# Windowed attention with a fused feed-forward product: attention row tiles by head pair, sums in one phase, and another order of the first loads

## The chip, the cores and the metric

One core of one Trainium2 chip runs the whole program. The metric is the device time of one execution in microseconds (us). "Span" is the length of the profiled execution, which is 1 to 2 us below the time of the same execution.

## The reference

Attention in a window of 32 tokens on either side, for 8 batches of 8 heads with 576 tokens of 64 elements, and then a feed-forward block over all 4,608 tokens:

```python
def _attn_ref(q, k, v):                                  # (8, 8, 576, 64) each
    scores = scale * np.matmul(q, k.transpose(0, 1, 3, 2))
    mask = np.abs(pos[:, None] - pos[None, :]) <= 32
    scores = np.where(mask, scores, -1000000000.0)
    ...                                                  # softmax over the last axis
    return np.matmul(attn, v)

def _moe_ref(x, w_in, w_out):                            # x (4608, 512), w_in (512, 2048), w_out (2048, 512)
    h = x @ w_in
    g = np.where(h >= 1, h, np.where(h <= -1, 0.0, (h + 1) ** 2 / 4.0))
    return g @ w_out
```

`x` is the output of the attention with the heads side by side, so no row of the first product can start before the attention of its token is done.

## The kernel before

The program is a list of steps in a fixed order. Step `a` computes one eighth (256 columns) of the first product for a tile of 256 tokens, `hp`; ScalarE and VectorE turn it into `gT`; and `LAG` steps later four matmuls of the second product, `op`, use it. The eight batches' attention is put between `hp` and `op` of chosen steps. There are 144 steps with an `hp`, and `LAG` more that have only `op`.

Q and K must have their 64 elements on the partitions. For batch 0 rows of nine tokens are loaded ("long" rows) and transposed on TensorE; for all others rows of one token are loaded and the DMA engines transpose them:

```python
    def load_long(b, qd):                     # 9 tokens of 64 elements in a run
        for src, dst, nm in ((q, qn, "qn"), (k, kn, "kn")):
            ...
            nc.gpsimd.dma_start(out=dst[b][:, qd], in_=rows.rearrange("h (x j) d -> x h (j d)", j=NC))

    def load_nat(b, t):                       # one token of 64 elements in a run
        ...
        for h in range(2):
            nc.gpsimd.dma_start(out=x[:, :, h], in_=src[b, NY * h:NY * h + NY].rearrange("y s d -> (y s) d")
                                .rearrange("(u p) d -> p u d", p=128))

    def xpose(b, t):                          # transpose by DMA
        nc.sync.dma_start_transpose(out=..., in_=(qn, kn)[t][b].rearrange("p u h d -> p (u h d)"))
    ...
    load_long(0, 0)
    load_long(0, 1)
    load_nat(0, 2)
    load_w_in(0, 512)
    load_w_in(512, DFF)
    for t in range(3):
        load_nat(1, t)
    for n in range(4):
        load_w_out(n)
    ...
    loads, xps = {}, {7: [(1, 0)], 8: [(1, 1)]}          # batch 1's DMA transposes in steps 7 and 8
```

The weighted sums of V (`nm`) and the row sums (`dn`) are made of 64x64 matmuls, with the two halves of the partitions ("row tiles") adding into the same PSUM banks. So they go in two phases, and a VectorE copy of one element (`scr`) keeps the second phase behind the first:

```python
    def part(ps, col):
        nc.vector.tensor_copy(scr[64:65, 0:1], ps[64:65, col:col + 1])
    ...
        def phase(first):
            s = list(sums(0 if first else 1, first))
            ...
            for f in s[:2] + list(rows(1 if first else 0, first)) + s[2:]:
                f()
            if first:
                part(nm, hi - lo - 1)
```

A step, in program order:

```python
        # the sums' first phase stands before hp if the step has no scores, else after it
        hp = ps_h.tile([128, 2, TB], FP, name="hp", tag="hp")
        for j in range(2):
            for kk in range(4):
                nc.tensor.matmul(hp[:, j], w_in[...], xT[:, kk, r0:r0 + TB], start=kk == 0, stop=kk == 3)
        nc.scalar.activation(rr, hp, AF.Relu, scale=0.5, bias=0.5)
        nc.vector.tensor_max(hp, hp, rr)
        nc.vector.scalar_tensor_tensor(gT[t][:, 2 * f:2 * f + 2], rr, 1.0, hp, op0=ALU.min, op1=ALU.mult)
        # scores of a later head, the sums' second phase, ln and exp of the row sums
        for x in range(4 * (a - LAG), 4 * (a - LAG) + 4):
            nc.tensor.matmul(op, gT[...], w_out[:, ff], ...)
```

The softmax here doesn't subtract the row's maximum and nothing guards it: scores larger than these inputs give would overflow.

Of the kernel before, what the change touches and what calls it, by code (L numbers as in the profile page):

```python
# [15 lines left out]
def kernel(  # L16
# [19 lines left out]

# [9 lines left out]
    PAD = 32  # L46

    const = ctx.enter_context(tc.tile_pool(name="const", bufs=1))
    nat = ctx.enter_context(tc.tile_pool(name="nat", bufs=2))
    ktp = ctx.enter_context(tc.tile_pool(name="ktp", bufs=3))  # L50
    ptp = ctx.enter_context(tc.tile_pool(name="ptp", bufs=5))
    pt8p = ctx.enter_context(tc.tile_pool(name="pt8p", bufs=2))
# [3 lines left out]
    osp = ctx.enter_context(tc.tile_pool(name="osp", bufs=2))  # L56
    ps_h = ctx.enter_context(tc.tile_pool(name="ps_h", bufs=2, space=bass.MemoryType.PSUM))
    ps_o = ctx.enter_context(tc.tile_pool(name="ps_o", bufs=2, space=bass.MemoryType.PSUM))
    ps_s = ctx.enter_context(tc.tile_pool(name="ps_s", bufs=2, space=bass.MemoryType.PSUM))
    ps_n = ctx.enter_context(tc.tile_pool(name="ps_n", bufs=1, space=bass.MemoryType.PSUM))  # L60
    ps_d = ctx.enter_context(tc.tile_pool(name="ps_d", bufs=1, space=bass.MemoryType.PSUM))
# [4 lines left out]
    mask4 = const.tile([128, 512], BF, name="mask4")  # L66
    mask8 = const.tile([128, 2 * TAIL], BF, name="mask8")
# [6 lines left out]
    V, P = nc.vector, nc.gpsimd  # L74
# [4 lines left out]
    def load_long(b, qd):  # L79

        for src, dst, nm in ((q, qn, "qn"), (k, kn, "kn")):
            if qd == 0:
                dst[b] = nat.tile([128, 2, 2, S], BF, name=nm, tag=nm)
            rows = src[b].rearrange("(h y) s d -> h (y s) d", h=2)[:, 2 * qd * S:2 * qd * S + 2 * S]
            nc.gpsimd.dma_start(out=dst[b][:, qd], in_=rows.rearrange("h (x j) d -> x h (j d)", j=NC))

    def load_nat(b, t):
        src, dst, nm = ((q, qn, "qn"), (k, kn, "kn"), (v, vn, "vn"))[t]
        x = dst[b] = nat.tile([128, NU, 2, D], BF, name=nm, tag=nm, bufs=3 if t == 2 else 2)
        for h in range(2):  # L90
            nc.gpsimd.dma_start(out=x[:, :, h], in_=src[b, NY * h:NY * h + NY].rearrange("y s d -> (y s) d")  # L91
                                .rearrange("(u p) d -> p u d", p=128))

    def load_w_in(f0, f1):
        f = slice(f0, f1)
        for h in range(2):
            nc.gpsimd.dma_start(out=w_in[64 * h:64 * h + 64, :, f],
                                in_=moe_w_in.rearrange("(h y d) f -> h d y f", h=2, d=64)[h][:, :, f])
# [5 lines left out]
    nc.scalar.preload_act_table_set("natural_log_exp_and_others")  # L104
    load_long(0, 0)
    make_identity(nc, ident)

    nc.gpsimd.memset(mask1, 1.0)
    for h in range(2):
        r = slice(64 * h, 64 * h + 64)  # L110
        nc.gpsimd.affine_select(out=mask1[r], in_=mask1[r], compare_op=ALU.is_ge, fill=0.0, base=0,
                                channel_multiplier=-1, pattern=[[1, 128]])
        nc.gpsimd.affine_select(out=mask1[r], in_=mask1[r], compare_op=ALU.is_ge, fill=0.0, base=64,
                                channel_multiplier=1, pattern=[[-1, 128]])
    load_long(0, 1)
    nc.vector.memset(ones, 1.0)
    for t in qTs:
        nc.vector.memset(t[:, 0:PAD], 0.0)
    for m, n, w in ((mask4, 4, 128), (mask8, 2, TAIL)):
        nc.vector.tensor_copy(m.rearrange("p (n j) -> p n j", n=n),  # L120
                              mask1[:, 0:w].rearrange("p (n j) -> p n j", n=1).to_broadcast([128, n, w]))
    load_nat(0, 2)
    load_w_in(0, 512)
    load_w_in(512, DFF)
    for t in range(3):
        load_nat(1, t)
    for n in range(4):
        load_w_out(n)


    qj, kj, kT = {}, {}, {}

    def relay(b, qd, t, eng):

        src, dst, nm = ((qn, qj, "qj"), (kn, kj, "kj"))[t]
        if qd == 0:
            dst[b] = gtp.tile([128, 2, NC, 2, D], BF, name=nm, tag="gT")
        eng.tensor_copy(dst[b][:, qd].rearrange("p j h d -> p h j d"),
                        src[b][:, qd].rearrange("p h (j d) -> p h j d", d=D))

    def qT(b):
        return qTs[b % 3][:, PAD:]

    def tpose(b, qd, t, part, copy):

        if t == 1 and b not in kT:
            kT[b] = ktp.tile([128, NY * S], BF, name="kT")
        j0, j1 = ((0, 5), (5, 9))[part]
        src = (qj, kj)[t][b]
        ps = ps_h.tile([128, 5, 128], BF, name="tp", tag="hp")  # L150
        for j in range(j0, j1):
            nc.tensor.transpose(ps[:, j - j0], src[:, qd, j].rearrange("p h d -> p (h d)"), ident)
        o = qT(b) if t == 0 else kT[b]
        copy(o.rearrange("d (y p j) -> d y p j", p=64, j=NC)[:, 2 * qd:2 * qd + 2, :, j0:j1],
             ps[:, :j1 - j0].rearrange("d j (g p) -> d g p j", g=2))

    def xpose(b, t):

        if t == 1:
            kT[b] = ktp.tile([128, NY * S], BF, name="kT")  # L160
        o = qT(b) if t == 0 else kT[b]
        nc.sync.dma_start_transpose(out=o.rearrange("d (u p) -> d u p", p=128),  # L162
                                    in_=(qn, kn)[t][b].rearrange("p u h d -> p (u h d)"))
# [3 lines left out]
    def half(n):  # L167
        return slice(64 * (n % 2), 64 * (n % 2) + 64)

    HD = (slice(0, 64), slice(64, 128))  # L170

    def scores(i, eng):
        b, y = divmod(i, NY)
        p = pt[i] = ptp.tile([128, 2, 512], BF, name="pt")
        ps = [ps_s.tile([128, 512], FP, name="sc", tag="sc") for _ in range(2)]
        for c in range(8):
            for h in range(2):
                nc.tensor.matmul(ps[h][half(NC * y + c), 128 * (c // 2):128 * (c // 2) + 128],  # L178
                                 kT[b][HD[h], S * y + 64 * c:S * y + 64 * c + 64],
                                 qTs[b % 3][HD[h], PAD + S * y + 64 * c - 32:PAD + S * y + 64 * c + 96],  # L180
                                 start=True, stop=True)
        for h in range(2):
            nc.scalar.activation(p[:, h], ps[h], AF.Exp, scale=D ** -0.5)  # L183
            eng.tensor_mul(p[:, h], p[:, h], mask4)  # L184

    def scores8(b, eng):
        p = pt8[b] = pt8p.tile([128, 2, 2 * TAIL], BF, name="pt8")
        ps = [ps_s.tile([128, 512], FP, name="sc", tag="sc") for _ in range(2)]
        for y in range(NY):
            for h in range(2):  # L190
                nc.tensor.matmul(ps[h][half(y), TAIL * (y // 2):TAIL * (y // 2) + TAIL],
                                 kT[b][HD[h], S * y + 512:S * y + 576],
                                 qTs[b % 3][HD[h], PAD + S * y + MAIN:PAD + S * y + S], start=True, stop=True)
        for h in range(2):
            nc.scalar.activation(p[:, h], ps[h][:, :2 * TAIL], AF.Exp, scale=D ** -0.5)
            eng.tensor_mul(p[:, h], p[:, h], mask8)

    def mm(o, w, x, **kw):
        return nc.tensor.matmul(o, w, x, skip_group_check=True, **kw)  # L199

    scr = const.tile([128, 8], FP, name="scr")

    def part(ps, col):

        nc.vector.tensor_copy(scr[64:65, 0:1], ps[64:65, col:col + 1])  # L205

    muls, spare = [], [False]

    def banks(alt):
        if alt and spare[0]:  # L210
            nm, dn = (ps_o.tile([128, 512], FP, name=n, tag="op") for n in ("nm", "dn"))
        else:
            nm, dn = ps_n.tile([128, 512], FP, name="nm"), ps_d.tile([128, 512], FP, name="dn")
        spare[0] = not spare[0]
        return nm, dn

    def finish_pv(nm, dn, n, out_ap, shape):
        lr = smp.tile([128, MAIN], FP, name="lr", bufs=1)
        rc = smp.tile([128, MAIN], FP, name="rc")
        nc.scalar.activation(lr[:, :n], dn[:, :n], AF.Ln)  # L220
        nc.scalar.activation(rc[:, :n], lr[:, :n], AF.Exp, scale=-1.0)  # L221
        muls.append(lambda: nc.vector.tensor_mul(out_ap, shape(nm[:, :n]), shape(rc[:, :n])))  # L222

    def pv(i, lo=0, hi=MAIN, alt=False):

        b, y = divmod(i, NY)
        nm, dn = banks(alt)
        def sums(par, first):
            R = half(y + par)
            n = 0  # L230
            for c2 in range(4):
                q0, q1 = 128 * c2 - 32 + 64 * par, 128 * c2 + 96 + 64 * par
                a0, a1 = max(0, q0, lo), min(q1, hi)
                if a0 >= a1:
                    continue
# [224 lines left out]
```

## Time and profile before

| | before |
|---|---|
| time, median (lowest to highest of 4) | 363.94 us (363.13 to 365.18) |
| span | 362.0 us |
| first `hp` | 26.98 us |
| step 10 begins | 67.24 us |
| step 143, the last with an `hp`, begins | 343.97 us |
| mean granted clock of TensorE, as the profile has it | 0.971 |

The profile's clock records begin only at 40.5 us in this run. The mean above and the row `PEclk` count the time before as full speed, although the first eight `hp` matmuls took 1.89 us there and 1.05 later: early on, read the clock from the matmuls' own times.

The prediction below reads the slices, the waits and the timeline. Beside them, this is the page's first part (busy time of each engine, its share of the span, its instructions) and the two VectorE groups that every step has (line, engine, operation, shapes and count, then busy time and mean ns, then the idle time before them and what ended it):

```profile
PE 303.8 (84%) x3227; PEld 202.6 (56%) x3268; DVE 245.1 (68%) x410; ACT 190.6 (53%) x353; POOL 124.7 (34%) x127
...
L409 DVE TENSOR_TENSOR hp<-hp,rr 128x512 f32<-128x512 f32 x144 | 100.7, 699 | 43.4 <-ACT rr L408 40.3
L410 DVE SCALAR_TENSOR_TENSOR gT<-rr,hp 128x512 bf16<-128x512 f32 x144 | 98.8, 686 | 5.0
```

TensorE is busy 84% of the span, but that average hides two stretches: the slices show it nearly full from 85 us on and half idle before. VectorE needs 0.699 + 0.686 = 1.385 us for every step, while TensorE needs 1.735 in a step without attention.

### The profile page before, as it was taken

Reading aid. Unit: us, or ns where it says so; the run is one execution under the profiler, and the core shown is the slowest. Engines: PE = TensorE matmul, PEld = TensorE weight load, DVE = VectorE, ACT = ScalarE, POOL = GpSimd, SP = SyncE. Lnnn points to the kernel's source line nnn. Section 1 sums busy time; section 2 is a strip of 40 time slices with the busy share of each in tenths; the row PEclk is TensorE's granted clock in tenths of the full one; section 3 lists DMA queues with packets and bytes.
Section 4 is the critical chain, followed back from the end, with each engine's and each line's share of the span. In section 5 each row is a group of like instructions: output and inputs, shape, how many; then the busy total and the mean of one; then the engine's idle time right before and its main releaser. Section 6 shows DMA issues by size and latency. Waiting matters only on the chain.

```text
span 362.0 us, 7810 instructions
## 1 busy us (share of the span) xinstructions
PE 303.8 (84%) x3227; PEld 202.6 (56%) x3268; DVE 245.1 (68%) x410; ACT 190.6 (53%) x353; POOL 124.7 (34%) x127
## 2 busy tenths in 40 slices
PE   1555830649999999999999999999999999999995
PEld 1333520336666666666666666666666666666642
DVE  2554660385788777778787877877878777788730
ACT  2464320373766657555655667567556665534421
POOL 8834121000963258313921394159313421000000
PEclk9999995598999999999999999999999999999999
DMA  7999999990998019970995099829940000100011
GB/s 105 177 193 151 124 175 92 139 163 0 88 166 165 31 49 152 117 161 29 134 190 94 29 147 111 189 38 130 181 101 32 30 31 31 56 34 29 32 72 72
DMA packets 144292, 36.54 MB, mean 101 GB/s; under 512 B 135553, under 2 KB 139137, under 8 KB 144257
## 3 DMA queue, kind: packets, MB, share of 16 engines
q0 software_dynamic: 106368, 18.35, 72.6%
q1 hardware_dynamic: 37888, 17.70, 25.0%
q8 instruction: 25, 0.41, 0.5%
q14 instruction: 11, 0.08, 0.1%
HBM read 36.70 MB, written 9.44 MB: 127 GB/s over the span
## 4 chain that ended last, share of the span: by engine, by line
PE 62%; DMA 14%; POOL 9%; DVE 5%; issue 4%; ACT 3%; SPq 2%; ACTq 0%; POOLq 0%
PE op L422 29%; PE hp L400 27%; DMA kT<-kn 9%; DMA qn<-in_q_dram 5%; PE nm L199 4%; SPq L162 2%; POOL vn L91 2%; POOL pt L184 2%; DVE hp L409 2%; POOL qn L91 2%; ACT rr L408 2%; DVE gT L410 1%; POOL kn L91 1%; DVE scr L205 1%; PE dn L199 1%
## 5 line engine op out<-in xcount | busy, mean ns | idle before, releaser
L400 PE MATMUL hp<-xT,w_in 128*128 128x256 bf16 x1152 | 155.2, 280 | 3.4 <-DVE gT L410 3.4
L408 ACT ACTIVATE rr<-hp 128x512 f32<-128x512 f32 x144 | 86.0, 597 | 115.4 <-PE hp L400 108.2
L422 PE MATMUL op<-w_out,gT 128*128 128x512 bf16 x535 | 138.5, 379 | 4.9 <-issue 4.1
L400 PEld LDWEIGHTS <-w_in 128*128 128x128 bf16 x1152 | 113.7, 100 | 48.6 <-DVE gT L410 6.0
L409 DVE TENSOR_TENSOR hp<-hp,rr 128x512 f32<-128x512 f32 x144 | 100.7, 699 | 43.4 <-ACT rr L408 40.3
L410 DVE SCALAR_TENSOR_TENSOR gT<-rr,hp 128x512 bf16<-128x512 f32 x144 | 98.8, 686 | 5.0
L184 POOL TENSOR_TENSOR pt<-pt,mask 128x512 bf16<-128x512 bf16 x48 | 54.6, 1161 | 117.0 <-ACT pt L183 117.0
L422 PEld LDWEIGHTS <-gT 128*128 128x128 bf16 x576 | 53.8, 98 | 42.6 <-issue 0.4
L183 ACT ACTIVATE pt<-sc 128x512 bf16<-128x512 f32 x64 | 34.7, 594 | 22.8 <-PE sc L178 22.6
L199 PE MATMUL nm<-pt,vn 64*64 64x128 bf16 (+2 forms) x656 | 33.8, 224 | 15.4 <-DVE xT L222 11.7
L199 PEld LDWEIGHTS <-vn 64*64 64x64 bf16 x656 | 24.0, 113 | 27.7 <-issue 25.5
L222 DVE TENSOR_TENSOR xT<-nm,rc 128x480 bf16<-128x480 f32 (+3 forms) x44 | 25.8, 592 | 19.7 <-ACT rc L221 15.6
L199 PE MATMUL dn<-pt,ones 64*64 64x64 bf16 (+5 forms) x272 | 33.1, 304 | 1.1 <-DVE xT L222 0.4
L178 PE MATMUL sc<-qT,kT 64*64 64x128 bf16 x512 | 14.8, 234 | 18.9 <-DMA kT<-kn 17.1
L426 ACT COPY osb<-op 128x512 f32<-128x512 f32 x36 | 21.0, 583 | 16.9 <-PE op L422 16.9
L221 ACT ACTIVATE rc<-lr 128x480 f32<-128x480 f32 (+3 forms) x44 | 24.3, 552 | 1.4
L178 PEld LDWEIGHTS <-kT 64*64 64x64 bf16 x512 | 12.4, 116 | 20.6 <-DMA kT<-kn 17.5
L220 ACT ACTIVATE lr<-dn 128x480 f32<-128x480 f32 (+3 forms) x44 | 23.1, 525 | 0.3
L91 POOL DMA_DIRECT2D kn<-in_k_dram x14 | 17.1, 1232 | 14.3 <-DMA vn<-in_v_dram 13.8
L91 POOL DMA_DIRECT2D vn<-in_v_dram x16 | 19.6, 1239 | 3.9 <-DMA w_out<-in_moe_w_out_dram 3.7
L184 DVE TENSOR_TENSOR pt<-pt,mask 128x512 bf16<-128x512 bf16 x16 | 6.5, 422 | 18.4 <-ACT pt L183 18.1
L91 POOL DMA_DIRECT2D qn<-in_q_dram x14 | 17.3, 1242 | 1.9 <-DMA kn<-in_k_dram 1.2
(33 smaller groups left out, 66.8 us busy)
## 6 DMA issues: line engine op xcount, KB each, us to landing
out_dram<-osb SPq DMA_DIRECT2D x36, 256.0 KB, 2.1
qn<-in_q_dram POOLq DMA_DIRECT2D x16, 288.0 KB, 6.8
kn<-in_k_dram POOLq DMA_DIRECT2D x16, 288.0 KB, 8.2
vn<-in_v_dram POOLq DMA_DIRECT2D x16, 288.0 KB, 10.2
w_out<-in_moe_w_out_dram POOLq DMA_DIRECT2D x4, 512.0 KB, 31.2
w_in<-in_moe_w_in_dram POOLq DMA_DIRECT2D x2, 768.0 KB, 13.5
w_in<-in_moe_w_in_dram POOLq DMA_DIRECT2D x2, 256.0 KB, 8.4
qT<-qn SPq DMA_TRANSPOSE x7, 5.1
```

What stands on the lines that cost most here:

```text
L91: nc.gpsimd.dma_start(out=x[:, :, h], in_=src[b, NY * h:NY * h + NY].rearrange("y s d -> (y s) d") .rearrange("(u p) d -> p u d", p=128))
L178: nc.tensor.matmul(ps[h][half(NC * y + c), 128 * (c // 2):128 * (c // 2) + 128], kT[b][HD[h], S * y + 64 * c:S * y + 64 * c + 64], qTs[b % ...
L183: nc.scalar.activation(p[:, h], ps[h], AF.Exp, scale=D ** -0.5)
L184: eng.tensor_mul(p[:, h], p[:, h], mask4)
L199: return nc.tensor.matmul(o, w, x, skip_group_check=True, **kw)
L221: nc.scalar.activation(rc[:, :n], lr[:, :n], AF.Exp, scale=-1.0)
L222: muls.append(lambda: nc.vector.tensor_mul(out_ap, shape(nm[:, :n]), shape(rc[:, :n])))
L400: nc.tensor.matmul(hp[:, j], w_in[:, kk, 256 * f + 128 * j:256 * f + 128 * j + 128], xT[:, kk, r0:r0 + TB], start=kk == 0, stop=kk == 3)
L408: nc.scalar.activation(rr, hp, AF.Relu, scale=0.5, bias=0.5)
L409: nc.vector.tensor_max(hp, hp, rr)
L410: nc.vector.scalar_tensor_tensor(gT[t][:, 2 * f:2 * f + 2], rr, 1.0, hp, op0=ALU.min, op1=ALU.mult)
L422: nc.tensor.matmul(op, gT[tt // 2][:, ff, 128 * (tt % 2):128 * (tt % 2) + 128], w_out[:, ff], start=ff == 0, stop=ff == 2 * NF - 1)
```

## The change

The intent is fourfold.

1. A row tile now belongs to a head pair (`a`), and each pair has its own PSUM bank. No bank is shared by row tiles, so the sums go in one phase, without the VectorE copy.
2. Batch 1's Q and K come in runs of nine tokens and are transposed on TensorE. Batches 0 and 1 are loaded by halves of their tokens, the first half of batch 0 as fp32 from the SP and ScalarE queues. Batch 2 is transposed on TensorE too. DMA transposes start with batch 3.
3. `LAG` falls from 14 to 10, and attention visits are placed anew.
4. Matmuls on zeros fill TensorE's idle time in the start, to keep its clock up.

Smaller edits come with these: a visit (a step's share of attention) now takes 224 or 256 tokens of four heads instead of 480 tokens of two, one exponential covers 1,024 columns instead of 512, and some of the first ten `hp` use the banks of `op`.

```diff
-    load_long(0, 0)
+    q32, k32 = (early.tile([128, 2, S], FP, name=nm) for nm in ("q32", "k32"))
+    load_long(0, 0, 0, nc.sync, q32)
+    load_long(0, 0, 1, nc.scalar, k32)
 ...
-    load_nat(0, 2)
-    load_w_in(0, 512)
-    load_w_in(512, DFF)
-    for t in range(3):
-        load_nat(1, t)
-    for n in range(4):
-        load_w_out(n)
+    load_v(0)
+    load_w_in(0)
+    load_long(0, 1, 0)
+    load_long(0, 1, 1)
+    for n in range(1, 4):
+        load_w_in(n)
+    load_w_out(0)
+    load_long(1, 0, 0)
+    load_long(1, 0, 1)
+    load_w_out(1)
+    load_v(1)
+    load_w_out(2)
+    load_w_out(3)
+    load_long(1, 1, 0)
+    load_long(1, 1, 1)
 ...
-    def part(ps, col):
-        nc.vector.tensor_copy(scr[64:65, 0:1], ps[64:65, col:col + 1])
 ...
+    def sums(b, y1, lo, hi, pool=ps_n):
+        bb = two_banks(pool)                  # [128, 2, 512] fp32: one bank per head pair a
+        ...
+        for n, (c, c0, c1, p) in enumerate(todo):
+            o = D0 if c is None else 0
+            for a in range(2):
                 for h in range(2):
+                    nc.tensor.matmul(bb[HD[h], a, o + c0:o + c1], ones[HD[a]] if c is None else vn[b][HD[a], c, h],
+                                     p(a, h), start=n == 0, stop=True, skip_group_check=True)
 ...
+    def keep_warm(n, pool, tag):
+        z = pool.tile([128, 512], FP, name="z", tag=tag)
+        for _ in range(n):
+            nc.tensor.matmul(z, warm[:, :128], warm, start=True, stop=True)
 ...
-    LAG = 14
+    LAG = 10
 ...
+    at(2, None, (0, (0, 1), (0, 2), (2, 4)))          # scores alone
+    at(3, None, (0, (1, 2), (0, 2), (2, 4)))
+    at(4, None, (0,))
+    at(5, (0, 0, TB, MAIN), None)                     # sums alone
+    at(6, (0, 1, TB, MAIN), None)
+    at(7, (0, 0, MAIN, S), None)
 ...
+    for a, b, half in ((0, 0, 1), (8, 1, 0), (15, 1, 1)):         # transposes on TensorE
+        for t in range(2):
+            tps[a + t] = [(b, 2 * half + part, t) for part in range(2)]
+    for n in range(3):
+        tps[20 + n] = [(2, n, t) for t in range(2)]
```

## The prediction

> **What bounds the kernel now.** The kernel is one core. Each of its 144 steps makes a 256-column piece of the first matmul (8 matmuls, `hp`), turns it into `gT` on ScalarE and VectorE, and, some steps later, does 4 matmuls of the second product (`op`). Attention for later batches is slipped between `hp` and `op`. I first read the page's 40 slices (9.05 us each).
>
> ```profile
> PE   1555830649999999999999999999999999999995
> ...
> PEclk9999995598999999999999999999999999999999
> DMA  7999999990998019970995099829940000100011
> GB/s 105 177 193 151 124 175 92 139 163 0 88 166 165 31 49 152 117 161 29 134 190 94 29 147 111 189 38 130 181 101 32 30 31 31 56 34 29 32 72 72
> ```
>
> From slice 10 (about 85 us) TensorE is full; before it TensorE is half idle while DMA is full, and the granted clock halves in slices 7 and 8. So there are two regimes. The waits and the chain of waits name the first; the TensorE timeline dates it.
>
> ```profile
> PE sc L178 <- DMA kT<-kn: 17.1, 2, 16.3
> ```
>
> ```profile
> 12.71 17.75 DMA qn<-in_q_dram
> 30.54 7.34 SPq L162
> 38.00 28.62 DMA kT<-kn
> ```
>
> ```profile
> 26.98 1.89 PE L400 MATMUL hp<-xT,w_in 128*128 128x256 bf16 x8
> ...
> 49.31 1.05 PE L400 MATMUL hp<-xT,w_in 128*128 128x256 bf16 x8 [0.81 <-DVE gT L410]
> 66.66 0.64 PE L178 MATMUL sc<-qT,kT 64*64 64x128 bf16 x16 [16.31 <-DMA kT<-kn]
> ```
>
> The reader sees: the first `hp` starts at 26.98 and at half speed (1.89 against 1.05 us); ten steps are done by 51; then 16.3 us pass until the DMA transpose of batch 1's K, itself 28.6 us long among other loads, lands. The first `op` comes at 84.6. At 85.60 begins the sixteenth step, at 344.13 the last: 128 steps in 258.5 us. A step without attention takes 0.87 + 0.865 = 1.735 us, 222 us for 128. The remaining 36.5 us belong to 31 attention visits, some 1.15 each. One of them:
>
> ```profile
> 95.32 1.04 PE L400 MATMUL hp<-xT,w_in 128*128 128x256 bf16 x8
> ...
> 96.29 0.23 PE L199 MATMUL nm<-pt,vn 64*64 64x96 bf16 x2
> ...
> 96.51 0.40 PE L178 MATMUL sc<-qT,kT 64*64 64x128 bf16 x16
> ...
> 96.77 0.16 DVE L205 COPY scr<-nm 1x1 f32<-1x1 f32 x1
> ...
> 96.98 0.22 PE L199 MATMUL nm<-pt,vn 64*64 64x64 bf16 x2
> ...
> 97.53 0.81 PE L422 MATMUL op<-w_out,gT 128*128 128x512 bf16 x3 [0.16 <-issue]
> ...
> 98.18 1.04 PE L400 MATMUL hp<-xT,w_in 128*128 128x256 bf16 x8
> ```
>
> From `hp` to `hp` 2.86, so attention costs 1.12: 0.10 between `hp` (ends 96.19) and the first sums, 0.22 first phase, 0.2 scores, then until 96.98 the second phase waits for the one-element VectorE copy `scr` (ends 96.93), about 0.25; then 0.2 of sums and about 0.13 back to `op` (one `op` record is missing). Only about 0.65 of 1.12 is streaming.
>
> **What the Trainium skill says.** "TensorEngine Tiling (Array Packing)", Gotcha 1: row tiles that share a PSUM bank must be kept apart by software; and, under Key Properties, changing the tiling mode drains the array. The trace agrees: the `scr` copy is that separation, and the gaps of 0.10 and 0.13 lie at the mode changes. "TensorE: Matmul & The Clock Gate", Part 1: the array runs at half clock until it has been busy some 3.4 us, and again after idling as long. The trace agrees in effect: eight `hp` matmuls take 1.89 at 27 us, 1.05 from 42 us on, and again 1.89 after the stall. "DMA: Bandwidth & Descriptors", Specifications: under 512 bytes per piece the line rate is missed. The windows agree: 217 GB/s from 18 to 20 us when weights load, 148 from 98 to 100 us when Q, K and V load in 64-element rows.
>
> **The change part by part.**
>
> *Loads.* Batch 1's Q and K now come in runs of nine tokens and are transposed on TensorE; so do batch 0's, the first half as fp32 from the SP and ScalarE queues at once. Batch 2 is transposed on TensorE too. In written bytes, at 215 GB/s for wide rows and 150 for token rows: fp32 half 3 us (1.18 MB, my estimate at the read rate of the cast loads, twice 215), V of batch 0 3.9, first w_in quarter 2.4, second half of Q and K 2.7, rest of w_in 7.3, w_out in four parts 9.8, batch 1's Q and K 5.5, its V 3.9: 38.5 us. From 2 us that ends at 41. Before, token-wise batches 1 and 2 and four DMA transposes came into the same stretch. The last of it, batch 1's second half, is wanted at step 15. So the 16.3 us stall should go.
>
> *Start.* Halves land at about 5 us; cast (0.7), transposes (0.7), copies (0.75), the same for K, put the first scores near 10 us; three exponentials (1.0, 0.6, 1.0; one 512-wide takes 0.59) and masks (0.7) end near 13.4; sums, logarithm, exponential (0.6 each) and multiplication (0.66) put the first full `hp` at 15.5, 11.5 us earlier. V of batch 0 (about 10 us) and the first w_in (13) are in time. The zero matmuls (32 of 512 columns) fill gaps only and keep the clock up.
>
> *Steps 0 to 9*, without `op`. VectorE: 10 x (0.70 + 0.69) = 13.9, plus score masks 1.8 and multiplications 1.8: 17.5. ScalarE: 6 + 8 transpose copies x 0.74 + exponentials 2.5 + Ln/Exp 3.2 = 17.6. They alternate as the limit, so 20 us.
>
> *Sums in one phase, one bank per head pair.* No `scr`. All four 64x64 quadrants run together, as the scores do now ((0.40 - 0.22) / 15 = 12 ns from start to start, four per 128 columns). Per quadrant a visit streams 832 columns (tokens 0 to 224), 1024 (224 to 480) or 640 (tail): two, two and one per batch, 4352 columns at 2.4 per ns: 1.8 us. Scores 4 x 0.22 + 0.09 = 1.0. Mode changes 5 x 0.23 = 1.15. Sum 4.0 us per batch against 5.7.
>
> *Steps 10 to 153* (`op` lags 10 instead of 14): 134 x 1.735 + 10 x 0.865 = 241.1. Attention 7 x 4.0 = 28, plus 0.7 for visits that have only scores or only sums. TensorE transposes in steps 15, 16 and 20 to 22: about 5. Small waits, 2. Together 276.8. The ending (last `op` to the end) stays 4.0.
>
> *Sum.* 15.5 + 20 + 276.8 + 4.0 = 316.3 of span; the timed median before is 1.2 above its span, so 317.5. I add 1.5 for unforeseen waits: **319 us**. Of the gain of 44, 11 come from the earlier start, 20 from steps 0 to 9 with the stall (step 10 at 35.5 instead of 67.2), 12 from the cheaper sums and some 7 from steps 10 to 14, which had no `op` and partly half clock; transposes take back about 5.
>
> **The rivals.** (1) *A load wait takes the stall's place.* 24 small SWDGE issues of Q and K rows and eight of V take GpSimd's time: 0.73 us for 256 rows, 1.23 for 2304, so about 32 us in all from 3.5 to 36. Each wait of 1 us adds 1. If the ring is full, as where GpSimd now waits 12.8 us before `kn`, w_out parts 2 and 3 could come after steps 12 and 13: 325 to 332. For: all margins are 2 to 6 us. Against: the data finish by 41 in my sum. (2) *Smaller matmuls issue slower than they stream*: 132 matmuls of sums per batch against 112. At 25 ns each they would take 3.3 instead of 1.8 us, +10: 329. Against: scores now start every 12 to 14 ns with their weight loads hidden. (3) *VectorE or ScalarE becomes the bound.* VectorE 1.39 per step plus 0.66 per visit is under TensorE's 1.735 plus 0.8. ScalarE needs 0.6 + 2.2 in a visit, TensorE 2.55, but steps between have slack. +3 if it binds. (4) *The stall was hidden anyway*: then only sums gain, about 350. The idle TensorE before 66.66 speaks against it.
>
> **Range and chances.** Start ±3, steps 0 to 9 ±4, the long stretch ±5, mostly upward: 310 to 331. For less than 2% (above 356) most of the stall would have to return; I give 0.03, slower 0.01.
>
> **What would show it.** First `hp` at 14 to 18 us and its eight matmuls at about 1.05; step 10 with the first `op` at 33 to 40; no TensorE wait over 3 us for a DMA; no half clock after 15 us; a visit with scores and sums adding 0.8 to 0.9 instead of 1.12; DMA quiet near 41 us but for batch 2. The prediction is wrong if `hp` after 40 us waits for `gT`, if transposes wait for Q and K of batch 1, or if `op` waits for w_out.

## The result, and the profile after

The changed kernel takes **328.94 us** (median of 4, 328.39 to 330.11) against 363.94 us. The ratio is 0.904, with a 95% interval of 0.900 to 0.908. Every ratio in this document is the mean time of one kernel's fast runs over that of the kernel before in the same rounds, so it is not quite the ratio of the medians quoted beside it. The time lies inside the predicted range of 310 to 331 and 10 us above the predicted point.

The four rows of the page's slices that answer to those of before (each slice is now 8.19 us):

```profile
PE   4788599999999999999999999999899999999995
...
PEclk9699799999999999999999999999999999999999
DMA  9999999991946999599972996619990010000011
GB/s 161 172 173 180 153 188 120 168 141 35 106 106 113 97 152 134 106 105 136 76 154 56 108 165 117 106 56 140 144 188 35 2 65 34 34 32 34 32 66 64
```

TensorE is full from the sixth slice (41 us) instead of 85. Two dents are left: the second slice (8 to 16 us) with a granted clock of 0.6, and the fifth (33 to 41 us), where busy time falls to 5 tenths and the clock to 0.7. DMA still runs full for nine slices, so the first 74 us are still crowded with loads, but TensorE no longer waits for them. The waits of TensorE say the same; these are the first six lines (line and tile, who was waited for, then us in total, times, and the longest):

```profile
PE op L421 <- issue: 5.6, 35, 0.2
PE tp L184 <- DVE qb L302: 4.8, 1, 4.8
PE bb L261 <- DVE xT L273: 2.5, 2, 2.1
PE hp L403 <- DVE xT L276: 1.8, 1, 1.8
PE bb L207 <- ACT kT L185: 1.7, 3, 0.6
PE hp L403 <- DVE gT L409: 1.3, 7, 0.3
```

The first line is no wait: of 576 `op` matmuls 535 are recorded, but all 576 of their weight loads, and the missing records are nearly all of the first `op` of a step with attention, just where this gap lies. No DMA is in the list. The largest single wait is for the cast of the fp32 Q half (`qb`), which in turn waits for a load. The timeline of the start (start, duration, engine, what, and in brackets the idle time before it and what ended that):

```profile
0.81 1.80 SPq L87 DMA_DIRECT2D q<-in_q_dram  x4
...
8.94 0.49 DVE L302 CAST qb<-q 128x640 bf16<-128x640 f32 x1 [7.23 <-DMA q<-in_q_dram]
...
9.49 1.14 PE L184 MATMUL tp<-ident,qb 128*128 128x128 bf16 x9 [4.80 <-DVE qb L302]
```

Q was issued at 0.81 us and could be used at 8.9. The first `hp` begins at 20.88. Then the dent in the fifth slice, in TensorE's timeline:

```profile
31.44 1.05 PE L403 MATMUL hp<-xT,w_in 128*128 128x256 bf16 x8
34.55 0.33 PE L261 MATMUL bb<-pt,ones 64*64 64x224 bf16 x4 [2.06 <-DVE xT L273]
...
35.40 1.89 PE L403 MATMUL hp<-xT,w_in 128*128 128x256 bf16 x8
...
39.97 1.03 PE L403 MATMUL hp<-xT,w_in 128*128 128x256 bf16 x8 [1.80 <-DVE xT L276]
```

Here the steps 5, 6 and 7 each have sums, and all three use the one pair of banks for sums. Step 6's sums (34.55) wait until VectorE has multiplied those of step 5 out of the bank, 2.06 us; the `hp` of step 7 after it runs at half speed (1.89 against 1.05 us for the same eight matmuls; the trace's clock record has half clock from 34.67 to 38.08 us); and the `hp` of step 8, the first of the second token tile, waits for the last multiplication of batch 0, 1.80 us.

Last, a visit of attention in the full stretch, the same kind of step as the one shown of before:

```profile
94.12 1.05 PE L403 MATMUL hp<-xT,w_in 128*128 128x256 bf16 x8 [0.16 <-DVE gT L409]
95.09 0.30 PE L261 MATMUL bb<-pt,ones 64*64 64x256 bf16 x4
...
95.56 0.40 PE L207 MATMUL bb<-qT,kT 64*64 64x128 bf16 x16
96.12 0.81 PE L421 MATMUL op<-w_out,gT 128*128 128x512 bf16 x3 [0.16 <-issue]
96.77 1.04 PE L403 MATMUL hp<-xT,w_in 128*128 128x256 bf16 x8
```

From `hp` to `hp` it is 2.65 us here, and 2.48 to 2.56 in most such steps, against 2.86 before. There is no gap for a copy: the 28 matmuls of the sums take 0.47 us from the first to the first score, with all four quadrants at work.

Where the 34.6 us of span went, by the first matmul of the steps:

| stretch | before | after | gain | predicted after |
|---|---|---|---|---|
| start to first `hp` | 26.98 | 20.88 | 6.1 | 15.5 |
| steps 0 to 9 | 40.26 | 22.29 | 18.0 | 20 |
| step 10 to the end | 294.8 | 284.2 | 10.6 | 280.8 |
| - of it, steps 10 to 14 | 18.4 | 11.9 | 6.4 | |
| - of it, steps 15 to 142 | 258.4 | 258.0 | 0.4 | |
| - of it, step 143 to the end | 18.0 | 14.3 | 3.7 | |
| span | 362.0 | 327.4 | 34.6 | 316.3 |

So most of the gain lies where the stall was, and the prediction's miss of 11 us of span is spread: 5.4, 2.3 and 3.4.

The three rows of its parts show two more things. From step 15 to step 142 almost nothing was gained, although a visit is 0.3 us cheaper: the TensorE transposes of batches 1 and 2 (some 3 us in steps 15, 16 and 20 to 22), two steps with scores alone (1.5 us) and late steps (some 3 us, below) take it back. And steps 10 to 14 gained 6.4 us, although with the smaller `LAG` four of them now carry an `op`, which is what the end lost. Before, the sums of steps 12, 13 and 14 follow one another and wait 5.0 us in all (67 to 86 us) until VectorE frees their one pair of banks; after, that wait is 0.4 us (43 to 56 us). This is the new placement of the visits. No run tests it alone, but from step 10 to step 15 e12, with the old placement, still takes 18.2 us, and e11, with the new one and two phases, 13.1.

### The profile page after: what moved, and what is told of

The parts are those of the page before. It is cut to its first block, busy times and chain, and to the rows that moved or that the text cites. A ratio compares the mean times of both kernels' runs of the same rounds, so it can differ in the third digit from the quotient of the medians.

```text
span 327.4 us, 8334 instructions
## 1 busy us (share of the span) xinstructions
PE 301.0 (92%) x3527; PEld 201.6 (62%) x3570; DVE 233.1 (71%) x357; ACT 195.1 (60%) x321; POOL 136.2 (42%) x133
## 4 chain that ended last, share of the span: by engine, by line
PE 59%; issue 11%; ACT 10%; POOL 9%; DVE 7%; DMA 2%; SPq 0%; ACTq 0%; POOLq 0%; DVEq 0%
PE hp L403 25%; PE op L421 25%; PE bb L261 5%; POOL pt L215 4%; ACT pt L214 3%; DVE hp L408 2%; DVE gT L409 2%; POOL vn L103 2%; DMA q<-in_q_dram 2%; PE bb L207 2%; ACT rr L407 2%; POOL qn L95 2%; ACT lr L267 2%; POOL kn L95 1%; ACT osb L425 1%
## 5 line engine op out<-in xcount | busy, mean ns | idle before, releaser
L215 POOL TENSOR_TENSOR pt<-pt,mask 128x1024 bf16<-128x1024 bf16 x24 | 51.3, 2139 | 99.9 <-ACT pt L214 83.8
L421 PEld LDWEIGHTS <-gT 128*128 128x128 bf16 x576 | 53.1, 98 | 41.8
L214 ACT ACTIVATE pt<-bb 128x1024 bf16<-128x1024 f32 (+1 forms) x33 | 33.1, 1011 | 5.7 <-PE bb L207 4.3
L273 DVE TENSOR_TENSOR xT<-bb,rc 128x512 bf16<-128x512 f32 (+1 forms) x32 | 21.0, 657 | 20.4 <-ACT rc L268 19.5
L425 ACT COPY osb<-op 128x512 f32<-128x512 f32 x36 | 20.9, 581 | 12.0 <-PE op L421 11.7
L103 POOL DMA_DIRECT2D vn<-in_v_dram x32 | 27.6, 896 | 0.0
L268 ACT ACTIVATE rc<-lr 128x512 f32<-128x512 f32 (+2 forms) x40 | 23.5, 587 | 1.3
L267 ACT ACTIVATE lr<-bb 128x512 f32<-128x512 f32 (+2 forms) x40 | 22.0, 550 | 3.7 <-PE bb L261 3.5
L261 PE MATMUL bb<-pt,ones 64*64 64x256 bf16 (+3 forms) x352 | 20.1, 260 | 3.6 <-DVE xT L273 2.5
L261 PE MATMUL bb<-pt,vn 64*64 64x128 bf16 (+3 forms) x712 | 18.9, 207 | 0.0
L261 PEld LDWEIGHTS <-ones 64*64 64x64 bf16 x352 | 11.2, 108 | 12.4 <-issue 11.3
L207 PE MATMUL bb<-qT,kT 64*64 64x128 bf16 x520 | 12.9, 218 | 2.7 <-ACT kT L185 1.7
```

Of the source, the lines that this page charges most:

```text
L103: nc.gpsimd.dma_start(out=x[64 * a:64 * a + 64, :, h], in_=v[b, y:y + 2].rearrange("y s d -> (y s) d") .rearrange("(c r) d -> r c d", r=64))
L214: A.activation(p, ps[:, :, :128 * n].rearrange(like, y=m), AF.Exp, scale=D ** -0.5)
L215: eng.tensor_mul(p, p, mask4[:, :256 * n].rearrange("p (h j) -> p h j", h=2).rearrange(like, y=m))
L261: nc.tensor.matmul(bb[HD[h], a, o + c0:o + c1], ones[HD[a]] if c is None else vn[b][HD[a], c, h], p(a, h), start=n == 0, stop=True, skip_g ...
L267: A.activation(lr[:, :, :D0], bb[:, :, D0:2 * D0], AF.Ln)
L421: nc.tensor.matmul(op, gT[tt // 2][:, ff, 128 * (tt % 2):128 * (tt % 2) + 128], w_out[:, ff], start=ff == 0, stop=ff == 2 * NF - 1)
```

## The experiments

Two questions had to be settled: how much of the gain comes from the form of the loads and how much from the one-phase sums (**theory**: mostly the stall, some 20 us, and 12 from the sums; **rival**: the stall would have been hidden, or the sums are what matters); and what the missing 10 us were. Three calls, each with all its kernels on one chip; the kernel before took 363.45 us (median of 7), 365.62 (of 11) and 363.23 (of 11) in them. Kernels whose name begins with "before" are edits of the kernel before, the others of the changed kernel. All twelve gave correct results.

### The form of the loads, alone on the kernel before: e1

```diff
-    for t in range(3):
-        load_nat(1, t)
+    load_long(1, 0)
+    load_long(1, 1)
+    load_nat(1, 2)
 ...
-    loads, xps = {}, {7: [(1, 0)], 8: [(1, 1)]}
+    loads, xps = {}, {}
 ...
+        if 4 <= a < 8:                        # at the end of steps 4 to 7
+            qd, t = divmod(a - 4, 2)
+            relay(1, qd, t, V)
+            for pp in range(2):
+                tpose(1, qd, t, pp, A if t == 0 else C)
```

> One part alone on the kernel before: batch 1's Q and K in runs of nine tokens and transposed on TensorE, nothing else. If the form of batch 1's loads is what made the 16.3 us stall, the stall goes, steps 10 to 14 run at full clock, and the time is 343 to 350. Rival: the queue is full of other loads anyway and the wait moves to V of batch 1, to w_out or to batch 2: 355 or more.

Measured: 367.89 us, ratio 1.0095 (1.0039 to 1.0151). A miss. Its waits of TensorE show why:

```profile
PE tp L153 <- DVE qj L139: 11.4, 3, 6.1
...
PE tp L153 <- DVE kj L139: 8.2, 4, 2.9
...
PE sc L179 <- DMA kT<-kn: 2.4, 1, 2.4
```

The 16.3 us wait for the DMA transpose is gone; 2.4 us of that kind remain, for a later batch. But each transposition now waits for a VectorE copy (`qj`, `kj`) issued just before it, and its result takes the bank that the next `hp` wants. Steps 4 to 7 took 5.5 to 6.4 us each, and step 10 began at 68.1 us, where it began before. The edit put a chain of VectorE, TensorE and ScalarE work in the place of the stall, so it does not say what the load's form is worth. It was repeated with the chain taken apart.

### The same with the chain taken apart: e12

The copies go into steps 2 to 5, each two steps ahead of its transposition, and the transpositions use the score banks, which are free in these steps.

```diff
+        if 2 <= a < 6:                        # at the start of the step
+            relay(1, *divmod(a - 2, 2), V)
 ...
+        if 4 <= a < 8:
+            qd, t = divmod(a - 4, 2)
+            for pp in range(2):
+                tpose(1, qd, t, pp, A if pp == 0 else C)
 ...
-        ps = ps_h.tile([128, 5, 128], BF, name="tp", tag="hp")
+        ps = (ps_h if b == 0 else ps_s).tile([128, 5, 128], BF, name="tp", tag="hp" if b == 0 else "sc")
```

> Batch 1's wide loads on the kernel before, once more, with the reorderings two steps ahead of the transposes and these in the score banks, so that the chain of reordering, transposes, copies and hp of the first form (each of steps 4 to 7 5.5 to 6.4 us) is loosened. If the load's form is worth about 17 us (as undoing it in the changed kernel cost), 345 to 352. Rival: the part alone is worth nothing there, because TensorE transposes and copies fill the time: 360 or more.

Measured: 351.08 us, ratio 0.9668 (0.9618 to 0.9718). Steps 4 to 7 took 2.2, 2.6, 2.6 and 1.6 us; step 10 began at 53.1 us instead of 67.2. So the form of batch 1's loads alone is worth 12 us on the kernel before, and e1's miss was its placement. "Form" is two things here, and in e2: long rows instead of rows of one token, and transposes on TensorE instead of by DMA. No run separates them.

### The form of the loads, undone in the changed kernel: e2

```diff
-    LONG, NAT = 2, 3
+    LONG, NAT = 1, 3
 ...
-    load_long(1, 0, 0)
-    load_long(1, 0, 1)
+    load_nat(1, 0)
+    load_nat(1, 1)
 ...
-    load_long(1, 1, 0)
-    load_long(1, 1, 1)
 ...
-    for a, b, half in ((0, 0, 1), (8, 1, 0), (15, 1, 1)):
+    for a, b, half in ((0, 0, 1),):
 ...
-    loads, xps = {}, {}
+    loads, xps = {}, {4: [(1, 0)], 5: [(1, 1)]}
```

> One part undone in the changed kernel: batch 1's Q and K by token rows and DMA transpose, as before, in the same place of the queue. If the form of the load is what matters, a wait of 5 to 12 us for a kT transpose comes back at step 10: 334 to 341. Rival: with the new start and order of the queue either form is in time: 328 to 331.

Measured: 346.54 us, ratio 0.9506 (0.9447 to 0.9565). Its timeline of TensorE, and its chain of waits (start, duration, what):

```profile
43.58 1.05 PE L401 MATMUL hp<-xT,w_in 128*128 128x256 bf16 x8 [0.79 <-DVE gT L407]
61.82 0.64 PE L205 MATMUL bb<-qT,kT 64*64 64x128 bf16 x16 [17.20 <-DMA kT<-kn]
```

```profile
21.31 13.66 DMA qn<-in_q_dram
35.05 6.68 SPq L187
41.84 19.94 DMA kT<-kn
```

For comparison, a K transpose by DMA in the quiet stretch of the kernel before, in its chain of waits:

```profile
153.87 1.50 SPq L162
155.47 4.57 DMA kT<-kn
```

Up to step 10 (43.6 us) nothing has changed; then the old stall is back, with the same three links as before: token-wise load, SP's DMA transposes, and a K transpose that takes 19.9 us among other loads where one in the quiet takes 4.57. The wait is longer than the 5 to 12 us expected. The span is 344.3, 16.9 above the changed kernel's. The rival "the stall was hidden anyway" is dead: undone in the changed kernel, the load's form costs 17 us.

### The one-phase sums, undone: e3 and e11

First, two phases of matmuls as before (the head pairs keep their own banks, so the wait comes back and not the need for it), with the two one-element copies placed where the sums are called, after the step's own VectorE work:

```diff
-        for n, (c, c0, c1, p) in enumerate(todo):
-            o = D0 if c is None else 0
-            for a in range(2):
+        def phase(first):
+            for c, c0, c1, p in todo:
+                o = D0 if c is None else 0
+                a = int((c is None) == first)
                 for h in range(2):
                     nc.tensor.matmul(bb[HD[h], a, o + c0:o + c1], ...)
+            if first:
+                for a in range(2):
+                    V.tensor_copy(scr[64:65, a:a + 1], bb[64:65, a, a * D0:a * D0 + 1])
+        phase(True)
         def end():
+            phase(False)
```

> The wait put back in the changed kernel: sums in two phases (numerators of one head pair with denominators of the other), one-element copies by VectorE after the first, scores between. If the single phase is worth what the steps show (0.81 instead of 1.12 us per visit), some 33 visits cost 0.25 to 0.35 more each: 337 to 341. Rival: the wait hides behind the scores or the streams were the gain: 329 to 332.

Measured: 434.9 us, ratio 1.1916 (1.1834 to 1.1999), far slower than either kernel. The timeline of all engines in one visit:

```profile
152.72 0.28 PE L265 MATMUL bb<-pt,ones 64*64 64x224 bf16 x2
...
153.45 0.70 DVE L419 TENSOR_TENSOR hp<-hp,rr 128x512 f32<-128x512 f32 x1 [0.31 <-ACT rr L418]
154.19 0.69 DVE L420 SCALAR_TENSOR_TENSOR gT<-rr,hp 128x512 bf16<-128x512 f32 x1
...
154.88 0.23 DVE L270 COPY scr<-bb 1x1 f32<-1x1 f32 x2
155.17 0.28 PE L265 MATMUL bb<-pt,ones 64*64 64x224 bf16 x2 [1.85 <-DVE scr L270]
```

The first phase is done at 153.1, but the copies stand in VectorE's queue behind the step's 1.385 us of `hp` and `gT`, which themselves wait for ScalarE; so TensorE waits 1.85 us. Over the run it waits 72.0 us for `scr`, 38 times. The test is flawed: it measures the copy's place in the queue and not the phases. It was repeated as e11 with the sums ahead of the step's VectorE work, which is where the kernel before has its copy:

```diff
+        su, sc = ev.get(a, (None, None))
+        end = sums(*su) if su else None
+        if t < NB:
             rr = ewp.tile([128, 2, TB], FP, name="rr")
             ...
-        su, sc = ev.get(a, (None, None))
-        end = sums(*su) if su else None
```

> The two-phase sums once more, now with the one-element copies ahead of the step's own VectorE work, as the kernel before has it. If the single phase is worth the 0.3 us per visit seen in the steps, some 33 visits cost 0.2 to 0.4 each: 336 to 343. If the first form of this test (435 us) told the true cost of the wait, it stays over 400. Rival: under 332.

Measured: 346.77 us, ratio 0.9533 (0.9484 to 0.9582), above the 336 to 343 expected. One visit, with its scores between the two phases of sums:

```profile
92.39 1.04 PE L414 MATMUL hp<-xT,w_in 128*128 128x256 bf16 x8
...
93.56 0.40 PE L207 MATMUL bb<-qT,kT 64*64 64x128 bf16 x16
94.08 0.28 PE L265 MATMUL bb<-pt,ones 64*64 64x224 bf16 x2
...
95.27 1.04 PE L414 MATMUL hp<-xT,w_in 128*128 128x256 bf16 x8
```

From step 26 on a visit takes 2.83 to 2.98 us from `hp` to `hp`, 0.3 more than in the changed kernel, and the visits' sum is near the prediction: from step 10 to step 143 it takes 279.5 us against 269.9, so 9.6 (the prediction had 12). What I had not counted is the rest: its first `hp` comes 1.8 us later and its step 10 8.0 us later. TensorE waits 2.3 us until then for the copies themselves; the `hp` of steps 0, 1, 7, 8 and 9 take 1.75 to 2.73 us, where only those of steps 0 and 7 are so slow in the changed kernel. That the copies lie in the chain of the start, and that the longer idle time brought half clock, fits this but is argued. Together the one-phase sums are worth 17 us of span (344.9 against 327.4) against this form of two phases.

### Zero matmuls taken away: e4

```diff
         z = pool.tile([128, 512], FP, name="z", tag=tag)
-        for _ in range(n):
+        for _ in range(0):
             nc.tensor.matmul(z, warm[:, :128], warm, start=True, stop=True)
```

> The zero matmuls taken out of the changed kernel. If they keep the clock up, the sums of batch 0 and the first three or four steps run at half clock (8 hp matmuls 1.89 instead of 1.05 us): first hp about 21, step 4 about 2 to 4 us later, 330 to 333. Rival: they only cost (five of them stand before the K transposes for 2.1 us): 326 to 328.

Measured: 331.25 us, ratio 0.9079 (0.9015 to 0.9142). The first `hp` comes at 20.5 us, no later than with them, but steps 0 and 1 take 3.76 and 2.92 us instead of 2.49 and 1.60, and step 10 begins at 47.6 instead of 43.2. The profiled run was its slowest (333.34 us), so its span, 4.2 above the changed kernel's, overstates the effect; by the medians it is 1 to 2 us, and its interval overlaps the changed kernel's. The zero matmuls help by a little and how much is not settled.

### The changed kernel again: e5

> The changed kernel itself again, as the yardstick for the three small edits of the same call: 328 to 330.

Measured: 330.26 us, ratio 0.9043 (0.9016 to 0.9070), with the kernel before in 5 rounds. It is the yardstick for what follows; its step 8 begins at 39.7 and step 10 at 44.3.

### The missing 10 us: another bank for one sum, e6

```diff
-    at(6, (0, 1, TB, MAIN), None)
+    at(6, (0, 1, TB, MAIN, ps_s), None)
```

> Sums of step 6 in the score banks instead of the one pair of sum banks. If steps 6 to 8 (3.96 and 4.58 us instead of about 2) are long because three sums in a row share one pair of banks, so that each waits for logarithm, exponential and multiplication of the one before, the 2.06 us wait goes, the clock does not drop at 35 us, and 2 to 4 us are saved: 325 to 327. Rival: VectorE and ScalarE in order are the limit there: within 1 of the yardstick.

Measured: 328.9 us, ratio 0.8997 (0.8973 to 0.9022), 1.4 us below e5, between the two forecasts. Step 7 begins at 32.5 us instead of 35.2 in e5, so the wait for the bank is gone, but most of it comes back one step later:

```profile
PE hp L403 <- DVE xT L276: 3.2, 1, 3.2
```

Step 8 opens the second token tile and needs the product of all three sums. With the bank wait gone TensorE only reaches that point sooner, and waits 3.2 us for the last multiplication instead of 1.8. Half clock came all the same (the `hp` of steps 8 and 9 take 1.87 and 1.89 us). The bank was part of the reason; a second part may be that the sums are placed too late for step 8.

### Sums of batch 0 one step earlier: e9

```diff
-    at(4, None, (0,))
-    at(5, (0, 0, TB, MAIN), None)
-    at(6, (0, 1, TB, MAIN), None)
-    at(7, (0, 0, MAIN, S), None)
+    at(4, (0, 0, TB, MAIN), (0,))
+    at(5, (0, 1, TB, MAIN, ps_s), None)
+    at(6, (0, 0, MAIN, S), None)
```

> Batch 0's remaining sums at steps 4, 5 and 6 instead of 5, 6 and 7, the middle one in the score banks. If the gap ahead of step 8 is the chain sums, logarithm, exponential, multiplication behind VectorE's own work of step 7, it goes with one step more of slack, step 8 starts at 33 to 35 instead of 39.7 at full clock, and the time is 324 to 327, unless w_out and V of batch 1 (landing near 42 to 46) then stop steps 11 and 12: 327 to 329. Rival: no gain against 328.9 of the variant with the score banks alone.

Measured: 327.31 us, ratio 0.9007 (0.8970 to 0.9044); span 325.5. Step 8 begins at 36.7 us (39.97 in the changed kernel) and step 10 at 41.4 (43.2):

```profile
PE hp L402 <- DVE xT L276: 2.2, 1, 2.2
```

2.2 us of wait remain before step 8: Ln, Exp and the multiplication behind two steps of `gT` on VectorE. By ratio e9 cannot be told from e6 (0.9007 and 0.8997), so its rival stands; its gain is seen in the start of step 10 alone. In both, VectorE is busy 3.4 of the 3.4 us up to half clock (33.2 to 36.6 us in e6, 33.7 to 37.1 in e9), so e6's rival, that VectorE in order is the limit there, fits what remains. e6 and e9 place the excess of steps 0 to 9, 2.3 us over the prediction, in the sums' chain through banks and VectorE; how it divides is open.

### The start: fp32 halves, e7 and e8

Q and K of the first half as bf16 again, through GpSimd's queue like the other loads, so half the written bytes and no cast:

```diff
-    q32, k32 = (early.tile([128, 2, S], FP, name=nm) for nm in ("q32", "k32"))
-    load_long(0, 0, 0, nc.sync, q32)
-    load_long(0, 0, 1, nc.scalar, k32)
+    load_long(0, 0, 0)
+    load_long(0, 0, 1)
 ...
-        qn[0, 0] = cast(q32, "qb", 5)
-        kn[0, 0] = cast(k32, "kb", 5)
```

> The fp32 part undone: the first half of batch 0's Q and K comes as bf16 through GpSimd, without casts, masks made after V's issues. If twice the written bytes and the two casts are what delayed the start (q landed at 8.8 us, not at 5), q lands at 5.5 to 6.5, the first hp starts at 17 to 18.5 instead of 20.9, time 325 to 327. Rival: GpSimd's eight issues and the later V of batch 0 take it back: 328 to 331.

Measured: 330.92 us, ratio 0.9053 (0.9020 to 0.9086), the same as e5. The first `hp` begins at 18.3 us instead of 20.9, and then step 2 waits:

```profile
PE hp L399 <- DMA w_in<-in_moe_w_in_dram: 3.8, 2, 3.1
```

Step 2 is the first that needs the second quarter of `w_in`. It begins at 25.6 us here, at 25.0 in the changed kernel. So the fp32 form of the first halves neither gains nor loses: what it does to the first `hp` is hidden behind the loads that step 2 needs.

Does V's traffic slow the fp32 halves? In e8 GpSimd waits for Q before it issues V:

```diff
+    hold = const.tile([128, 2], FP, name="hold")
+    P.tensor_copy(hold, q32[:, :, S - 1])
     load_v(0)
```

> fp32 kept; GpSimd waits for q before it issues V of batch 0. If the traffic of V (issued from 2.9 us) held q back, q lands at 6 to 7, the first hp comes 1.5 to 2.5 us earlier, 326 to 328. Rival: q and k are bound by their own bytes and issues: q still near 8.5 and V too late for the first sums: 329 to 333.

Measured: 333.67 us, ratio 0.9127 (0.9091 to 0.9163). The timeline has

```profile
8.71 0.49 DVE L304 CAST qb<-q 128x640 bf16<-128x640 f32 x1 [7.00 <-DMA q<-in_q_dram]
```

so with V out of the way Q came at 8.7 us instead of 8.9. The halves are slow by themselves: 1.18 MB in about 7 us is some 168 GB/s. With nothing else loading, the windows of e8 have 133 GB/s from 1 to 3 us, 216 from 3 to 5, 213 from 5 to 7 and 34 from 7 to 8.7. The theory that V's load slows them is wrong, its rival right. The later V and `w_in` cost 3 us.

### Both together: e10

e9's placement, with Q as bf16 through GpSimd first and K as fp32 split over the SP and ScalarE queues:

```diff
+    k32 = early.tile([128, 2, S], FP, name="k32")
+    load_long(0, 0, 1, (nc.sync, nc.scalar), k32)
+    load_long(0, 0, 0)
 ...                                          # and the edit of e9
```

> The same plus a mixed start: Q's first half as bf16 through GpSimd ahead of all else, K's as fp32 from the SP and ScalarE queues by halves. If the fp32 pair is bound by its own 1.18 MB (168 GB/s), half of it lands near 5, Q near 6, first hp at 17.5 to 19 and w_in's second quarter in time: 1 to 3 us under the shifted variant. Rival: loads are the limit from step 2 to 12, and an earlier start is only waited away: within 1 us of it.

Measured: 327.33 us, ratio 0.9008 (0.8970 to 0.9047), span 325.3, the same as e9. The first `hp` begins at 17.46 us, 3.4 sooner, and step 10 at 40.2, but the time is not on the clock at the end:

```profile
PE hp L401 <- DMA w_in<-in_moe_w_in_dram: 2.9, 1, 2.9
...
PE tp L182 <- DMA qn<-in_q_dram: 1.8, 1, 1.8
...
PE op L419 <- DMA w_out<-in_moe_w_out_dram: 1.1, 1, 1.1
```

Step 2 again begins when `w_in` lands (24.5 us), half clock follows (the `hp` of step 3 take 1.86 us), and an `op` waits for `w_out`. So once the stall is gone the first 45 us are, in the load orders tried, near the limit of their loads, and an earlier start is spent in waiting. e6, e9 and e10 have the lowest ratios (0.8997 to 0.9008), 0.4 to 0.5% below the changed kernel's and with intervals that overlap its own.

### What the runs add up to

| part undone or done alone | effect |
|---|---|
| batch 1's load form undone in the changed kernel (e2) | +16.9 us of span |
| batch 1's load form done alone on the kernel before (e12) | -12.7 us of span |
| one-phase sums undone (e11) | +17.5 us of span |
| zero matmuls undone (e4) | +1 to 2 us of time |
| fp32 halves undone (e7) | none |

Undone in the changed kernel, the two large parts cost about 17 us each. That this comes near the gain of 34.6 is no account of it: the first part alone gives 12.7 on the kernel before, the second was not tried there, and the table by stretches has gains that neither run explains (steps 10 to 14). The first `hp` that comes 6 us earlier belongs partly to the one-phase sums (1.8 us in e11), and partly to the load order. Load order, `LAG` and the placement of visits were not taken apart by any run.

## Why the prediction was right or wrong

**The stall: right.** It was predicted to go, and steps 0 to 9 with it to fall from 40 to 20 us; they fell to 22.3. e2 brings it back (17.2 us) and e12 takes it away on the kernel before. No TensorE wait for a DMA over 3 us: right. Step 10 began at 43.2 us, not at 33 to 40. The reason given, that the loads would be done by 41 us, was off: the last issue of the first group is at 47 us and DMA stays full to 74, because GpSimd's queue waits for earlier loads between its small issues, as rival 1 had it, and later batches follow. But none of that was wanted sooner by TensorE.

**The sums: right in kind and size.** A visit adds 0.75 to 0.82 us where 0.8 to 0.9 was predicted and 1.12 was before; e11 gives 9.6 us for the steps from 10 to 143 where 12 was predicted. What the working left out is that two phases also delay the start and the first steps: 8 us more in e11, which the prediction had under other heads.

**The start: wrong, the term "fp32 half 3 us".** It took 1.18 MB at twice 215 GB/s. They came at 168 GB/s, and in e8, alone, at no more than 216, the rate of the other wide loads and not twice it. So "halves land at about 5 us" became 8.9, and the first `hp` was 20.9 instead of 15.5, outside the 14 to 18 that was to show it and outside the 3 us allowed for the start. Its eight matmuls took 1.94 us and not 1.05, although the clock was full, for after two of them they waited 0.74 us for a multiplication. Waiting for the halves left TensorE idle from 4.7 to 9.5 us, after which the clock was granted at 0.57 from 9 to 15 us in the windows view and five zero matmuls between the transposes of Q and K took 2.13 us: so the zero matmuls did not keep the clock up through the wait. (From 15 to 30 us it was 1.00.) More important is a second omission: only the first quarter of `w_in` was checked for being in time. In e7 and e10 step 2 does not begin before 24.5 us, although the first `hp` comes at 18.3 and 17.5. With these load orders a first `hp` at 15.5 would not have made the predicted time.

**Steps 0 to 9: the term "20 us" is too small by 2.3.** It summed the busy time of VectorE and ScalarE and left out that the sums of three steps in a row share one pair of banks, and that step 8 needs them all. e6 takes away 1.4 us of it against e5; the wait for VectorE that remains is the term's other part. With the idle time came half clock at 35 us, so the check "no half clock after 15 us" fails there.

**Steps 10 to the end: 280.8 predicted, 284.2 measured.** Steps without attention at 1.735 us are right to the hundredth. (The prediction dates the last step of before at 344.13 us by the chain of waits; by the timeline, in which it dates the others, it is 343.97.) Attention was the term too small: it took 31.8 us (from `hp` to `hp`, over 1.74 for the step) where 28.7 was summed, 3.0 of it in the steps with scores alone (10, 11, 17 and 18). The transposes in steps 15, 16 and 20 to 22 took 3.3 instead of 5, waits and late steps 3.8 instead of 2. In steps 30 to 127 eight of the steps without attention took 2.0 to 2.2 us instead, because `hp` waited for VectorE to free its bank (the wait for `gT`, 7 times, 1.3 us in sum, each followed by a late start), and one visit waited 0.7 us for GpSimd's mask. That is rival 3 in small, and one of the signs by which the prediction was to be wrong, `hp` waiting for `gT` after 40 us: VectorE is not the bound, but has too little slack to be never late. In e11, with its longer visits, none of these steps is late.

**The sum.** The excess was 11.1 us of span. 1.5 had been added for unforeseen waits, and the median lies 1.6 above the span instead of 1.2, so the time is 9.9 over. All three stretches erred to the same side, the side on which the prediction had put most of its range. Rival 2 (matmuls of the sums issue slower than they stream) did not happen: 28 matmuls took 0.47 us, 17 ns each. Rival 4 is refuted by e2.

## What to carry to other kernels

A stall on a load is read by asking which form of load it waits for and what that competes with: here the same K transpose took 4.6 us in the quiet stretch and 28.6 in the crowded start, and loading long rows and transposing on TensorE removed it. Before you move a first matmul forward, list when each later step's loads land; an earlier start is worth nothing if the third step waits for its weights. When you put a small ordering instruction on an engine with long work of its own, place it before that work: the same copies cost 88 us more in the wrong place (e3 against e11). And read the gain by stretches: 0.3 us saved in each of 33 visits was spent again on work that the same change moved to TensorE.

## What the Trainium skill lacked or had wrong

- "TensorE: Matmul & The Clock Gate", Part 1, puts the return to half clock after about 3.4 us of idling. Here a wait of 2.06 us was enough: TensorE worked until 32.5 us, waited until 34.55, and the next eight `hp` matmuls took 1.89 us; in e9 a wait of 2.19 us was followed by 1.53. A wait of 1.80 us (before step 8) was not followed by half speed: 1.03. The trace's record has half clock from 34.67 to 38.08 us; in the 3.41 us before it TensorE was busy 1.35 us, so the stretch that brought it was not idle throughout. From 38.08 to 41.49 us it was busy 1.61 us, and the clock stayed full.
  The same part says that start-to-start times never fall below about 25 ns however few the columns. With four 64x64 quadrants at work, 16 score matmuls of 128 columns took 0.40 us, of which one is 0.22: 12 ns from start to start on average, in fours 3 to 4 ns apart, each four 55 to 60 ns after the one before. Part 3 of the same page has about 4 ns for tiles packed side by side, which this fits; the sentence in Part 1 is only too wide. The 25 ns of rival 2 is its figure.
- "TensorEngine Tiling (Array Packing)", Key Properties, says that a change of tiling mode drains the array and gives no price. Here a visit's first sums start 0.20 us after the last `hp` matmul, 31 times from 60 us on, where `hp` matmuls follow each other at 0.11: some 0.09 us for the change, an estimate from these two.
- "DMA: Bandwidth & Descriptors", section "Latency and other measured facts", gives 261 GB/s and more for DMA transposes. Here DMA moved 211 to 216 GB/s while the transposes of one batch's Q and K ran in the quiet stretch (154 to 160 us of the kernel before). From issue to landing K (0.59 MB as bf16) took 4.57 us, 129 GB/s with Q's still under way at first, and 28.62 us, 21 GB/s, among other loads. The page has no figure for a transpose that shares the engines, and that is the last link of the stall.
- No page that I read puts a price on the place of a small instruction in an engine's queue: a one-element copy behind two VectorE instructions made TensorE wait 1.85 us in the visit shown of e3, and 72.0 us in sum.
